# Landmark attention with a SiLU MLP: landmark scores as full-array products from batch 2 on, their exp in four pieces, exp(C) of batches 2 and 3 transposed by DMA, and a new order of the work

## The chip, the cores and the metric

The kernel runs on one core of a Trainium2 chip. The metric is the device time of one execution in microseconds (us). The core has a matrix engine (PE, with its weight loads shown as PEld), a vector engine (DVE), a scalar engine that evaluates functions by table (ACT), GpSimd (POOL) and a synchronisation engine (SP). In this kernel POOL issues the loads from memory, SP issues the DMA transposes and nearly all stores. Products land in PSUM, of which the kernel uses eight banks, and are copied from there by ACT or DVE.

## What is computed

Eight batches, eight heads, 576 positions, head size 64. Attention goes through 32 landmarks (means of 18 neighbouring positions); the result runs through a two-layer MLP with SiLU.

```python
m = 32; scale = 1.0 / np.sqrt(D)
q_lm = q.reshape(B, H, m, S // m, D).mean(axis=3)
k_lm = k.reshape(B, H, m, S // m, D).mean(axis=3)
A = sm(q, k_lm)            # sm: softmax of scale * a @ b.T
Bm = sm(q_lm, k_lm)        # 32 x 32 for each head
C = sm(q_lm, k)
Z = Bm.T / (norm_1(Bm) * norm_inf(Bm) + 1e-06)
for _ in range(6):
    Z = 2 * Z - Z @ Bm @ Z
x = A @ Z @ C @ v          # then heads are put side by side: 4608 x 512
h = x @ w_in               # 512 x 2048
out = (h * sigmoid(h)) @ w_out
```

## The kernel before

**Layout.** The heads of a batch lie in two groups (g = 0, 1) of four. A tile with heads and landmarks on its partitions has 4 x 32 = 128 of them. Positions are counted as landmark times 18 plus j.

**Order.** The kernel doesn't issue its work line by line. It describes some 1,500 pieces of work as `Op`s with a name such as `sb.3` (the landmark scores of batch 3), engines and estimated durations, dependencies, a priority and the PSUM banks needed. `Plan.run` (line 83) then places them engine by engine with a small model of durations, and the instructions are emitted in that order. The table `ORDER` (line 19) shifts priorities of single pieces by name; it is a list of numbers found by a search. Each engine works through its own list in order, so a piece that waits holds up all that stand behind it on that engine. While nothing else is ready in the first 45 us, PE gets filler products out of a zero tile (`zer`).

**Attention of one batch** (`attn`, line 540). For batches 0 to 2 (`NTR`) q and k are transposed on PE (`tr`, line 566) and copied out (`trc`); from batch 3 on SP transposes them by DMA (`xt`, line 590). The landmarks come from products with the identity in batches 0 and 1 (`lms`) and from batch 2 on from a tree of sums on DVE over the transposed q and k (`lra` to `lrd`, line 626), then a product with `fold` (`ltr`, line 646) and a copy into `lmT` (line 655). `fold` adds the halves and writes the sum to both halves of the partitions, so that `lmT` holds each landmark twice, on partitions 0 to 63 and 64 to 127.

`sb` (line 660) then makes the scores of the landmarks: for each group and each head one 32x32 product over 64 partitions, on a part of the array, eight in all. `pb` (line 677) takes the exp of these 128 x 64 scores in one ACT instruction. DVE sums, inverts and multiplies (`pbs`, `pbr`, `bmx`), PE sums columns (`csb`), DVE takes the norm; a block-diagonal square (`f0`) and six Newton steps follow (`ns` on PE, `nsd` on DVE, line 738).

`A` and `C` (lines 752, 797) are 16 products each with 64x32 parts of the array; ACT takes their exps (`Ax`, `Cx`, lines 768 and 813), PE sums those of A (`S`), ACT takes the logarithm and the exp of its negative (`Ln`, `Rs`), DVE multiplies (`etn`). The exps of C (tile `ce`) have to be transposed into `ct` before they multiply v. There are two ways: for `b < NCT`, with `NCT = 4`, PE transposes six blocks for each group (`ctm`, line 828) and ACT or DVE copies them out (`ctc`); for later batches SP transposes by DMA (`ct`, line 840). Then `cv` (line 848) makes C @ v on 96x64 parts, `zt` multiplies with Z, and `m` (line 895) with w_in on 64x32 parts.

**MLP.** `h` (line 927) multiplies `m` with the normalised exps of A, 16 blocks of 512 columns, with the remaining columns in `hx`; ACT applies SiLU (`g`, `gx`, line 940). The second layer (`layer2_pair`, line 1009) takes seven products `p1` to `p7` of 8 x 256 columns in place of eight, with sums of inputs on DVE (`ss`) and copies and additions of the results (`c1`, `c11`, `c22`, ...) into `ost`, from where SP stores. Pieces of the second layer stand between those of attention and of the first layer, so that PE has work while ACT is behind. SiLU and exp need different tables on ACT, so batches are taken in pairs: exps of batches 2 and 3, SiLU of 2 and 3, and so on.

**Transfers that exclude each other.** Loads come from POOL, for batch b+1 after batch b-1 has read its buffers. A DMA transpose is held back until the loads of the next v have landed (all but the last), and loads are held back for transposes. For C that is line 842, for the loads line 1125:

```python
xs + [prev.get("cv")] + v_ops.get(b + 1, [])[-2:-1], p0 + 20, lag=XLAG)]
...
gate = last[b - 1].get("xts", [])[-2:-1]
if b - 2 >= NCT:
    gate = gate + last[b - 2]["cts"][:1]
load_qk(b, 100.0 * b - 150, p["qk_read"], gate)
load_v(b, 100.0 * b - 149, [p["cv"]], gate)
```

Of the kernel before, what the change touches and what calls it, by code (L numbers as in the profile page):

```python
# [10 lines left out]
AF = mybir.ActivationFunctionType  # L11
# [5 lines left out]


ORDER = {
    "ns41.0": (259.18, 0), "mc21.0": (3218.2, 0), "mc31.0": (2171.9, 0), "tr19.1": (3337.5, 0),  # L20
    "lms0012.1": (4834.7, 0), "lms0112.1": (37.404, 0), "f0.1": (4487.7, 0),
    "Ax00.1": (418.45, 0), "Ax11.1": (120.61, 0), "etn1.1": (2471.6, 0), "Cx10.1": (6.1051, 0),
    "p3@5020.0": (591.27, 0), "tr10.2": (10.512, 0), "tr114.2": (-3277.8, 0),
    "lrb1.2": (92.182, 0), "ctm00.2": (-264.09, 0), "Cx11.2": (-1.6117, 0), "h12.1": (-10.003, 0),
    "c12@5100.0": (-2223.6, 0), "etn0.3": (-32.094, 0), "Ax10.3": (-1.1964, 0),
    "ctm10.3": (-212.55, 0), "ctc10.3": (1.228, 0), "mc01.3": (-72.297, 0), "m3.3": (-1035.6, 0),
    "p5@5200.0": (92.525, 0), "c12@5200.0": (-420.82, 0), "p3@5220.0": (291.71, 0),
    "c12@5220.0": (1822.7, 0), "wc.4": (385.62, 0), "m1.4": (5190.6, 0), "hx8.3": (-4.4068, 0),
    "p6@5300.0": (9579.2, 0), "p4@5300.0": (125.87, 0), "stf0.5": (79.994, 0), "C.5": (164.91, 0),
    "m3.5": (1570.1, 0), "p2@5400.0": (14.101, 0), "p4@5400.0": (-0.02249, 0),  # L30
    "Ax11.6": (-36.172, 0), "Cx10.6": (565.87, 0), "p6@5500.0": (-0.10422, 0),
    "ltr1.7": (-211.67, 0), "pbs.7": (230.47, 0), "bbd.7": (541.69, 0), "Rs0.7": (163.07, 0),
    "etn1.7": (-1755.9, 0), "hx0.6": (4199.5, 0), "p2@5740.0": (89.123, 0),
}


# [264 lines left out]
def act_us(n):  # L301
    return 0.06 + 0.00083 * n
# [6 lines left out]
def mm_us(n, count=1):  # L309
    return count * max(n / 2400 + 0.0025, 0.028)  # L310
# [3 lines left out]
def kernel(  # L314
# [9 lines left out]
    nc = tc.nc  # L324
    B, H, S, Dh = q.shape
    L = 32
    J = S // L
# [6 lines left out]
    NG = 2  # L334
# [3 lines left out]
    sc = 1.0 / float(Dh) ** 0.5  # L338
    SW = 128 + L
    NPE = 2  # L340
    NTR = 3
    MERGE = False
    WM = False
    NCT = 4
    XLAG = 3.0
    LOADS = "k1 q1 v0 w0 w1 w2 w3 o0 o1 o2 o3 v1".split()

# [8 lines left out]
    def bank(o, i=0):  # L356
        return banks[o.slot[i]]
# [33 lines left out]
    def mm(out_ap, lhsT, rhs, start=True, stop=True):  # L391
        nc.tensor.matmul(out=out_ap, lhsT=lhsT, rhs=rhs, start=start, stop=stop,  # L392
                         skip_group_check=True)
# [15 lines left out]
    A = P.add  # L409
# [74 lines left out]
    def consts(e):  # L484
# [13 lines left out]
        out=idb, in_=idb, compare_op=OP.is_equal, fill=0.0, base=0, pattern=[[-1, 128]],  # L498
        channel_multiplier=1), [c0], -99)
    for i, x in enumerate(LOADS):  # L500
        p, n = -95 + i, int(x[1])
# [38 lines left out]
    def attn(b):  # L540
        qk, qT, vs = qk_r[b % 2], qT_r[b % 2], v_r[b % 2]
        lm, lmT = lm_r[b % 2], lmT_r[b % 2]
        p0 = 100.0 * b
        prev = last.get(b - 1, {})
        prev2 = last.get(b - 2, {})
        me = last[b] = {}
# [3 lines left out]
        cr = b == 0  # L550
# [4 lines left out]
        if on_pe:  # L555
            blocks = {}
            me["qk_read"] = []
            for t in (1, 0):
                todo = [(g, jp) for g in range(NG) for jp in range(JP)]
                for i, n in STEPS[b]:  # L560
                    part = todo[i:i + n]

                    def tmm(e, t=t, part=part, key=(t, i)):
                        ps = bank(blocks[key]).bitcast(BF)
                        for n, (g, jp) in enumerate(part):
# [4 lines left out]
                    o = blocks[t, i] = A(f"tr{t}{i}.{b}", [("PE", mm_us(128, len(part)))], tmm,  # L570
                                         [qk_ops[b, t, part[0][0]], qk_ops[b, t, part[-1][0]], cid],
                                         p0 + 7 + (1 - t) * 0.5, psum=1)
# [9 lines left out]
        else:  # L582
# [3 lines left out]
            for t in (1, 0):  # L586
                for g in range(NG):
# [3 lines left out]
                            out=qT[:, t, g], in_=qk[:, t, g].rearrange("p j d -> p (j d)")),  # L591
# [10 lines left out]
        for t in (1, 0):  # L602
            if lm_pe:
                for g in range(NG):
                    for j0 in range(0, J, 6):
                        def lms(e, t=t, g=g, j0=j0):
                            ps = bank(me["lms", t])
                            for j in range(j0, j0 + 6):
# [3 lines left out]
                        o = A(f"lms{t}{g}{j0}.{b}", [("PE", mm_us(Dh, 6))], lms,  # L612
                              [qk_ops[b, t, g], cid] + ([] if first else [(me["lms_", t], 0.0)]),
                              p0 + 4 + 0.01 * j0 + 0.1 * g, psum=1 if first else 0, crit=True)
# [8 lines left out]
            else:  # L623
# [5 lines left out]
                if on_pe:  # L629
                    me["qk_read"] += blocks_of[t]  # L630
                x = lr("ra", 1024, red[:, :, 0:4], src[:, :, 0:4], src[:, :, 4:8],
                       qt_ops[t, 0] + qt_ops[t, 1] + tree[0])
                x = lr("rb", 512, red[:, :, 0:2], red[:, :, 0:2], red[:, :, 2:4], [x])
                x = lr("rc", 256, red[:, :, 0], red[:, :, 0], red[:, :, 1], [x])
# [22 lines left out]
        lmT_all = [lmT_ops[0], lmT_ops[1]]  # L657


        def sbm(e):  # L660
            ps = bank(me["sb"])
            for g in range(NG):
                for h in range(4):
                    mm(ps[L * h:L * h + L, g * L:(g + 1) * L], lmT[0:64, 0, g, L * h:L * h + L],
                       lmT[0:64, 1, g, L * h:L * h + L])
        ready = [l1_done.get(b - 2)] + prev.get("cts", []) + [prev.get("etn0"), prev.get("etn1")]
        if not cr:
            ready += sum(qt_ops.values(), [])
        ready = [x for x in ready if x is not None]
        me["sb"] = A(f"sb.{b}", [("PE", 0.2)], sbm, lmT_all + prev2.get("zt", []), p0 + (6 if cr else 11), psum=1,  # L670
                     tiled="q", crit=cr)
        pb, pbs = pb_r[b % 2], pbs_r[b % 2]
        bm, bmt = bm_r[b % 2][:, 0], bm_r[b % 2][:, 1]
        bbd = bbd_r[b % 2]
        sr = st_r[3 * (b % 2):3 * (b % 2) + 3]
        grp = "x0" if MERGE and b < 2 else f"x{b}"
        pb_op = me["pb"] = o = A(f"pb.{b}", [("ACT", act_us(64))],
                                 lambda e: nc.scalar.activation(
            out=pb, in_=bank(me["sb"])[:, 0:NG * L].rearrange("p (g l) -> p g l", g=NG),
            func=AF.Exp, scale=sc / (J * J)), [me["sb"]], p0 + 12, table="exp", group=grp,  # L680
            crit=cr).reads(me["sb"])
        pb_op.early = ready

        def chain(nm, us, emit, deps, prio=13):
# [505 lines left out]
```

## Time and profile before

| | |
|---|---|
| median of 4 runs | 250.94 us (250.38 to 252.05) |
| the profiled execution, its own time | 250.33 us |
| its span in the profile | 248.2 us |
| ACT, SiLU of the first layer (128 of 512 columns) | 65.8 us busy |
| PE, first layer (256 products of 512 columns) | 61.8 us busy |
| PE, filler products (94) | 15.8 us busy |
| PE, transposes of `ce` (48, batches 0 to 3) | 3.9 us busy |
| PE, landmark scores `sb` (64 products of 32 columns) | 1.8 us busy |
| ACT, exp `pb` (8) | 1.9 us busy, 233 ns each |
| SP, DMA transposes of `ce` into `ct` (8, batches 4 to 7) | 2.5 us from issue to landing, median |
| SP, DMA transposes of q and k (20) | 3.4 us from issue to landing, median |
| POOL, loads of v (24) | 12.1 us from issue to landing, median |

The span runs from the first to the last instruction of the program on the core; the execution's own time is 2.1 us longer. Busy times of PE overlap each other, since a product begins before the one before it has left the array: the distance from one start to the next tells what a product costs in a stream. The changes of ACT's table cut the span into stretches: SiLU of batch 0 begins at 33.7 us, the exps of batches 2 and 3 at 63.8, their SiLU at 89.8, the exps of 4 and 5 at 111.7, their SiLU at 137.1, the exps of 6 and 7 at 167.7, their SiLU at 190.5. The last product of PE ends at 244.3, after which the last results are added up and stored.

### The profile page before, as it was taken

What the parts mean: (1) busy time and instruction counts of PE and PEld (TensorE: products, weight loads), DVE (VectorE), ACT (ScalarE), POOL (GpSimd) and SP (SyncE); (2) the same over time, 40 slices, a digit from 0 to 9 for tenths busy, and PEclk for the clock granted to TensorE, in tenths of its full rate; (3) what the DMA queues carried; (4) which work ended last, traced back from release to release, by engine and by line L of the source; (5) the groups of instructions that cost most, each with busy time, mean ns of one, the idle gap of its engine ahead of it and who ended that gap; (6) DMA issues with size and microseconds to landing.
All of it is one profiled execution on the core that took longest, in us unless ns stands there. A gap on an engine that the chain in (4) does not pass through costs nothing.

```text
span 248.2 us, 7196 instructions
## 1 busy us (share of the span) xinstructions
PE 241.8 (97%) x2846; PEld 174.3 (70%) x2846; DVE 169.7 (68%) x430; ACT 182.8 (74%) x431; POOL 37.2 (15%) x63
## 2 busy tenths in 40 slices
PE   8999999999999999999999999999999999999993
PEld 6877665546877765567886564698876576688982
DVE  2376866596979886948999774489988384066421
ACT  2598998399886999996757979767679977822320
POOL 8436723200050022001300050000000000000000
PEclk9999999999999999999999999999999999999999
DMA  6999999999999699994995999674360033032333
GB/s 99 203 200 200 202 207 206 207 234 162 182 148 223 153 149 202 162 166 92 159 233 151 195 161 234 125 161 99 85 147 5 3 85 81 6 84 68 106 81 91
DMA packets 52482, 35.73 MB, mean 144 GB/s; under 512 B 33377, under 2 KB 43873, under 8 KB 52449
## 3 DMA queue, kind: packets, MB, share of 16 engines
q0 software_dynamic: 15264, 18.35, 44.7%
q1 hardware_dynamic: 36896, 16.66, 30.7%
q8 instruction: 22, 0.36, 0.6%
q10 hardware_dynamic: 288, 0.26, 0.4%
q14 instruction: 12, 0.09, 0.1%
HBM read 36.70 MB, written 9.44 MB: 186 GB/s over the span
## 4 chain that ended last, share of the span: by engine, by line
PE 86%; DMA 6%; ACT 3%; DVE 2%; issue 1%; POOL 0%; DVEq 0%; POOLq 0%; ACTq 0%
PE ps L392 83%; DMA qT<-qk 4%; DMA qk<-in_q_dram 3%; PE ps L566 2%; ACT ln L778 1%; DVE red L626 1%; ACT ln L782 1%; PE ps L828 1%; ACT ct L402 1%; ACT et L768 1%; ACT L940 1%; POOL qk L445 0%; DVE ost L1063 0%; ACT gm L940 0%; DVE ost L404 0%
## 5 line engine op out<-in xcount | busy, mean ns | idle before, releaser
L392 PE MATMUL ps<-etn,m 128*128 128x512 bf16 (+1 forms) x512 | 69.3, 286 | 0.1
L940 ACT ACTIVATE gm<-ps 128x512 f16<-128x512 f32 x128 | 65.8, 660 | 1.1 <-PE ps L392 0.9
L392 PEld LDWEIGHTS <-gm 128*128 128x128 f16 x512 | 48.2, 98 | 11.4 <-issue 2.4
L392 PE MATMUL ps<-w_out_sb,gm 128*128 128x256 f16 (+1 forms) x392 | 53.5, 281 | 0.0
L392 PEld LDWEIGHTS <-m 128*128 128x128 bf16 x512 | 32.5, 98 | 24.5 <-issue 2.3
L402 ACT COPY ost<-ps 128x256 f32<-128x256 f32 (+1 forms) x57 | 22.1, 388 | 33.8 <-PE ps L392 32.2
L392 PEld LDWEIGHTS <-ss 128*128 128x128 f16 x408 | 38.9, 98 | 7.1 <-issue 1.5
L1063 DVE TENSOR_TENSOR ost<-ost,ps 128x256 f32<-128x256 f32 x51 | 21.3, 417 | 27.3 <-PE ps L392 21.4
L392 PE MATMUL ps<-wt,ss 128*128 128x256 f16 x272 | 34.0, 273 | 0.0
L738 DVE SCALAR_TENSOR_TENSOR st<-st,ps 128x320 bf16<-128x320 bf16 (+3 forms) x54 | 21.6, 406 | 8.6 <-PE ps L392 8.3
L404 DVE CAST m<-ps 128x512 bf16<-128x512 f32 x31 | 20.0, 684 | 5.0 <-PE ps L392 4.5
L402 ACT CAST m<-ps 128x512 bf16<-128x512 f32 x33 | 17.9, 602 | 4.2 <-PE ps L392 4.2
L392 PE MATMUL ps<-w_out_sb,ss 128*128 128x256 f16 x136 | 17.6, 273 | 0.0
L392 PE MATMUL ps<-zer 128*128 128x256 bf16 x94 | 15.8, 304 | 1.1 <-DVE zer L485 1.1
L451 POOL DMA_DIRECT2D qk<-in_k_dram x7 | 5.0, 715 | 77.9 <-DMA qT<-qk 36.3
L458 POOL DMA_DIRECT2D v<-in_v_dram x24 | 14.0, 591 | 18.0 <-PE ps L392 11.0
L813 ACT ACTIVATE ce<-ps 128x288 bf16<-128x288 f32 x32 | 12.8, 412 | 5.2 <-PE ps L392 5.2
L392 PE MATMUL ps<-wt,gm 128*128 128x256 f16 x120 | 15.6, 273 | 0.0
L392 PE MATMUL ps<-st 128*128 128x160 bf16 (+1 forms) x96 | 14.4, 224 | 0.1
L1028 DVE TENSOR_TENSOR ss<-gm 128x1024 f16<-128x1024 f16 x15 | 10.2, 685 | 5.2 <-ACT gm L940 5.2
L778 ACT ACTIVATE ln<-ps 128x288 f32<-128x288 f32 x32 | 12.0, 435 | 1.6 <-PE ps L392 1.4
L402 ACT COPY qT<-ps 128x640 bf16<-128x640 bf16 (+1 forms) x13 | 8.5, 695 | 5.9 <-PE ps L566 5.9
(90 smaller groups left out, 328.0 us busy)
## 6 DMA issues: line engine op xcount, KB each, us to landing
out_dram<-ost SPq DMA_DIRECT2D x138, 64.0 KB, 1.8
v<-in_v_dram POOLq DMA_DIRECT2D x24, 192.0 KB, 12.1
qk<-in_k_dram POOLq DMA_DIRECT2D x7, 576.0 KB, 8.2
qk<-in_q_dram POOLq DMA_DIRECT2D x7, 576.0 KB, 11.4
w_out_sb<-in_moe_w_out_dram POOLq DMA_DIRECT2D x4, 512.0 KB, 11.3
w_in_sb<-in_moe_w_in_dram POOLq DMA_DIRECT2D x4, 256.0 KB, 8.8
w_in_sb<-in_moe_w_in_dram POOLq DMA_DIRECT2D x8, 128.0 KB, 7.2
qk<-in_k_dram POOLq DMA_DIRECT2D x2, 288.0 KB, 4.3
```

What stands on the lines that cost most here:

```text
L392: nc.tensor.matmul(out=out_ap, lhsT=lhsT, rhs=rhs, start=start, stop=stop, skip_group_check=True)
L402: nc.scalar.copy(out=out, in_=in_)
L404: nc.vector.tensor_copy(out=out, in_=in_)
L451: lambda e, t=t, src=src: nc.gpsimd.dma_start(out=qk_r[b % 2][:, t].rearrange("p g j d -> p g (j d)"), in_=src[b].rearrange("(g h) (l j) d ...
L458: lambda e, a=a: nc.gpsimd.dma_start(out=v_r[b % 2][a * L:(a + 1) * L, :, :], in_=v[b].rearrange("h (l a x) d -> a l h (x d)", l=L, a=VA)[ ...
L566: nc.tensor.transpose(out=ps[:, n * 128:(n + 1) * 128], in_=qk[:, t, g, 2 * jp:2 * jp + 2, :].rearrange("p j d -> p (j d)"), identity=idb)
L738: nc.vector.scalar_tensor_tensor(out=s2[:, g0:g1, lo:SW], in0=s[:, g0:g1, lo:SW], scalar=2.0, in1=ps[:, 0:NG * SW].rearrange("p (g x) -> p ...
L778: lambda e, g=g, c=c, ln=ln: nc.scalar.activation(out=ln[:, c], in_=bank(me["S", g, c])[:, 0:HS], func=AF.Ln),
L813: nc.scalar.activation(out=ce[:, :, 0:VP].rearrange("p (i c) (a l) -> p c a i l", c=2, a=VA)[:, c], in_=bank(me["C"], 2 * g + c)[:, 0:HS]. ...
L940: lambda e, dc=dc, cell=cell: nc.scalar.activation(out=gm[:, dc, :], in_=bank(cell["o"]), func=AF.Silu),
L1028: lambda e, o_=o_[:, k], x=x[:, k], y=y[:, k], op=op: nc.vector.tensor_tensor(out=o_, in0=x, in1=y, op=op), dep, 850.0 + prio / 100)
L1063: nc.vector.tensor_tensor(out=out_, in0=x, in1=y, op=OP.add)
```

## The change

1. `SBF = 2`: from batch 2 on `sb` makes one full-array product for each group, `lmT[:, 0, g]` with `lmT[:, 1, g]`, 128 partitions by 128 x 128. That holds the scores of all pairs of heads of the group; those of the same head are the four 32x32 blocks on the diagonal. As each landmark stands twice on the partitions, the sums are twice as large.
2. `pb` then takes the exp of the four diagonal blocks with four ACT instructions of 32 partitions x 64 columns, with half the scale.
3. `NCT = 2`: batches 2 and 3 transpose `ce` by DMA from SP as batches 4 to 7 do. With that the loads of batches 4 and 5 have to wait for the first such transpose of batches 2 and 3, and these transposes for the v loads of batches 3 and 4.
4. `ORDER` is a new list.

```diff
-    "ns41.0": (259.18, 0), "mc21.0": (3218.2, 0), "mc31.0": (2171.9, 0), "tr19.1": (3337.5, 0),
...
+    "tr09.0": (11.858, 0), "f0.0": (2417.6, 0), "nsd20.0": (1178, 0), "stf1.0": (616.27, 0),
...
+    SBF = 2
     MERGE = False
     WM = False
-    NCT = 4
+    NCT = 2
...
+        whole = b >= SBF
+
         def sbm(e):
             ps = bank(me["sb"])
             for g in range(NG):
+                if whole:
+                    mm(ps[:, g * 128:(g + 1) * 128], lmT[:, 0, g], lmT[:, 1, g])
+                    continue
                 for h in range(4):
                     mm(ps[L * h:L * h + L, g * L:(g + 1) * L], lmT[0:64, 0, g, L * h:L * h + L],
                        lmT[0:64, 1, g, L * h:L * h + L])
...
-        me["sb"] = A(f"sb.{b}", [("PE", 0.2)], sbm, lmT_all + prev2.get("zt", []), p0 + (6 if cr else 11), psum=1,
-                     tiled="q", crit=cr)
+        me["sb"] = A(f"sb.{b}", [("PE", mm_us(128, 2) if whole else 0.2)], sbm, lmT_all + prev2.get("zt", []), p0 + (6 if cr else 11), psum=1,
+                     tiled=None if whole else "q", crit=cr)
...
+            for h in range(4):
+                r = slice(L * h, L * h + L)
+                nc.scalar.activation(
+                    out=pb[r], in_=ps[r, 0:256].rearrange("p (g x) -> p g x", g=NG)[:, :, r],
+                    func=AF.Exp, scale=sc / (2 * J * J))
+        pb_op = me["pb"] = o = A(f"pb.{b}", [("ACT", act_us(64) * (4 if whole else 1))], pbe,
+                                 [me["sb"]], p0 + 12, table="exp", group=grp, crit=cr).reads(me["sb"])
```

In the instruction lists of the two kernels PE has 36 weight loads of `lmT` less, 48 products of 32 columns less and 12 of 128 columns more; 24 transposes of `ce` less; 6 fillers less. ACT has 24 small exps in place of 6, one copy of `ct` in place of six, three more copies of `lmT` and three fewer of `qT`; DVE takes up most of what ACT gives away in copies. SP has four more transposes. POOL's list is the same. The order of pieces differs on every other engine.

## The prediction

> **What bounds the kernel now.** I read the page first, then the stretches between ACT's changes of table, then PE in order of time, and last the queues of SP and POOL.
>
> ```profile
> span 248.2 us, 7196 instructions
> PE 241.8 (97%) x2846; PEld 174.3 (70%) x2846; DVE 169.7 (68%) x430; ACT 182.8 (74%) x431; POOL 37.2 (15%) x63
> PE 86%; DMA 6%; ACT 3%; DVE 2%; issue 1%; POOL 0%; DVEq 0%; POOLq 0%; ACTq 0%
> ```
>
> The second line is busy time, the third the chain that ended last: PE carries it. A busy PE is modelled and overlaps itself, so it doesn't prove that PE streams. The stretches and the starts do (columns: stretch; its length, then PE, PEld, DVE, ACT, POOL busy; clock, DMA, GB/s):
>
> ```profile
> 0.00:34.35 34.35, 32.80 (x517) 24.96 (x518) 20.55 (x72) 24.71 (x62) 19.76 (x35) 1.00 1.09 183
> ...
> 61.50:88.40 26.90, 26.32 (x371) 20.34 (x369) 23.77 (x68) 22.25 (x60) 3.14 (x5) 1.00 0.98 167
> 88.40:110.40 22.00, 22.00 (x219) 12.84 (x217) 15.19 (x33) 21.92 (x44) 3.15 (x5) 1.00 1.06 186
> ...
> 189.20:244.30 55.10, 55.05 (x515) 42.35 (x513) 26.34 (x52) 31.06 (x67) 0.00 (x0) 1.00 0.23 61
> ```
>
> Up to 34 us PE looks busy only because 94 filler products (out of zer) stand there: the limit is the chain of batches 0 and 1, with ACT busy 24.7 of 34.4 us. From 34 to 244 us PE is the limit; in 88 to 110, the SiLU of batches 2 and 3, ACT is full as well.
>
> PE in order of time, batch 2 and its surroundings (start, length, instructions, idle before):
>
> ```profile
> 61.51 0.22 PE L392 MATMUL ps<-lmT 64*32 64x32 bf16 x8
> 61.66 1.05 PE L392 MATMUL ps<-w_out_sb,gm 128*128 128x256 f16 x8
> ...
> 67.42 0.50 PE L828 MATMUL ps<-idb,ce 128*128 128x128 bf16 x6
> 67.75 0.27 PE L392 MATMUL ps<-bbd 128*128 128x128 bf16 x2
> 67.86 0.50 PE L828 MATMUL ps<-idb,ce 128*128 128x128 bf16 x6
> 68.20 1.04 PE L392 MATMUL ps<-w_out_sb,gm 128*128 128x256 f16 x8
> 69.16 0.44 PE L392 MATMUL ps<-qT,lmT 64*32 64x288 bf16 x16
> 69.53 1.05 PE L392 MATMUL ps<-wt,ss 128*128 128x256 f16 x8
> ...
> 72.44 0.41 PE L392 MATMUL ps<-et,hmask 128*128 128x288 bf16 x2 [0.58 <-DVE st L738]
> ```
>
> The cost is the distance from start to start, not the length. Six transposes of ce: 0.33. Two full products of 128 columns (bbd): 0.11. The scores sb: 0.15 plus the entry into the tiled array; that entry shows at 68.20, where eight products take 0.96 up to a tiled run instead of the usual 0.87, so 0.09. An isolated sb thus costs 0.24. The last line is the largest stop after 34 us.
>
> The queues (SP, then POOL):
>
> ```profile
> 61.50 5.71 SPq L590 DMA_TRANSPOSE qT<-qk  x4
> 68.01 15.78 SPq L1005 DMA_DIRECT2D out_dram<-ost  x16
> 83.97 6.40 SPq L590 DMA_TRANSPOSE qT<-qk  x4
> ```
>
> ```profile
> 68.45 0.70 POOL L451 DMA_DIRECT2D qk<-in_k_dram  x1 [18.17 <-PE ps L828]
> 69.15 0.71 POOL L451 DMA_DIRECT2D qk<-in_q_dram  x1
> 71.94 1.74 POOL L458 DMA_DIRECT2D v<-in_v_dram  x3 [2.08 <-PE ps L392]
> ```
>
> The loads of batch 4 start at 68.45, those of its v at 71.94 (after cv of batch 2), and only at 83.97 does SP transpose batch 4's q and k: a transpose waits for the second load of v.
>
> **What the Trainium skill says.** "TensorEngine Tiling (Array Packing)", Key Properties: changing the tiling mode drains the array. The trace agrees: 0.09 us in, about 0.10 out. "TensorE: Matmul & The Clock Gate", Back-to-back issue gap: warm, N columns take N/2.4 + 2.5 ns; for 128 that is 56 ns, the trace has 0.11 us for two. "DMA: Bandwidth & Descriptors", Issuing engines are not separate DMA queues: all DMAs run on the same 16 engines and interleave; the DMA share of about 1 in the stretch from 61.5 to 88.4 fits. So four more transposes meet a busy DMA.
>
> **The change, part by part.**
>
> *Transposes of ce.* Batches 2 and 3 lose 4 groups of 6: 0.33 + 0.34 + 0.34 + 0.33 = 1.34 us of PE, all in the stretch where PE is the limit. Also 4 copies of ct (two took 1.50 us on ACT, so 3.0 us), which lay beside PE.
>
> *Scores as full products.* In three of the six batches (2, 3, 5) sb stands alone (0.24); in 4, 6 and 7 it joins a tiled run and costs 0.04. That is 0.84 against 6 x 0.11 = 0.66. But the new order breaks tiled runs elsewhere: from the first block of layer 1 that runs without fillers (h6 of batch 0) I count 66 changes of array mode before and 65 after. Costed that way: 6 x (0.11 - 0.04) = +0.42, less 0.10 for the one change. With -1.34, and -0.14 for one Newton step of batch 1 that now stands before h6, PE's work from h6 on falls by 1.16 us.
>
> *Four exp pieces.* One pb took 0.225 us. The skill's "ScalarE: Activation LUTs", What ACT_TABLE_LOAD costs, gives 186 ns plus 0.83 per column and an overlap of 93 ns between neighbours; with the trace's 0.225 I estimate 0.225 + 3 x 0.132 = 0.62 us. Bounds for four: 0.56 (they overlap as pb and the next exp at 12.78 and 12.92 do) and 0.90 (no overlap). 0.4 us longer per batch, in front of sum, reciprocal, product and csb on PE: some 1.7 us from pb to csb. Behind pb on ACT wait the first exps of C or A. The least PE work between sb and csb in the new order is 4.1 us (batch 3; before 2.5), so it is covered: 0. If the cover fails it costs 6 x 0.4 = 2.4.
>
> *ct by DMA for batches 2 and 3.* New waits: SP's ct of batch 3 waits for the second v load of batch 4; behind it on SP stand the q and k transposes of batch 4 and eight stores. The loads of batch 4 wait for the first ct of batch 2 (about 70.5: its exps end near 68, and a ct lands 2.5 us after issue), so 2 us later; the v loads follow cv of batch 2, now about 74.5 to 75 against 71.56. Loads and stores took 15.5 us from 68.45 to 83.97, so v is there at about 86; at the median of 12.1 us from issue to landing of v, at 88. Then the second ct of batch 3 lands 1.25 + 2.5 us later: 89.8 to 91.9. PE reaches cv of batch 3 at about 91.6: from h6 on I added, in the new order, each block's usual distance in the trace (0.43 for one h, 0.87 for one product p, 0.14 for a Newton step, 0.645 for cv, 0.1 for each change of mode), which gives 91.0, plus 0.6 for stops. So the wait lies between 0 and, with v's longest landing of 14.7, 3 us; I take 0.4. Batches 4 and 5 do the same already, without a stop on PE.
>
> *Order.* Start: 88 fillers instead of 94 (-0.66) and 0.34 more real work before h6: -0.3. ACT has there one ct copy and three qT copies less and one lmT more, about 2.1 us; if all of that is on the path the start gains 2.1, if not, and batch 0's later Newton chain (h0 stands 1.06 later) counts, it loses 0.7. The stop of 0.46 us before A of batch 4, where DVE waited for batch 5's transposes (DMA qT<-qk in the chain, 108.5 to 113.2), goes: that reduction now stands on DVE behind the norm of batch 4. The stop at 72.44 stays: it comes from batch 3's transposes, bound by loads that do not move.
>
> Sum against the profiled execution: -1.16 - 0.3 - 0.46 + 0.4 = -1.5; span 248.2 to 246.7, its own time 250.33 to 248.8. The median of the runs shown, 250.94, lies 0.6 above that execution, so 249.4.
>
> **Rivals.** (A) Forecast, 249.4. (B) The ACT work taken from the start is all on its path: -2.1 instead of -0.3, 247.6. For it: ACT is nearly unbroken from 13 to 32 us. Against it: only six fillers fewer. (C) The order's gain returns as new short stops elsewhere and only the transposes remain, partly: 250.5. For it: ACT and PE are both full in 88 to 110. (D) Slower: v of batch 4 lands late, so ct and cv of batch 3 stop PE for 3 us; the q and k transposes of batch 4, behind ct on SP, then stop DVE in front of copies of m of batch 3 for 1 more: -1.9 + 4.0 gives 253.0. From 88 us on, each us of later landing costs one; slower than 0.5% from about 91. For it: DMA is full there. Against it: batch 5 ran so with 1.5 us to spare. That sb or pb do nothing of what they say is excluded by the instruction lists.
>
> **How the numbers follow.** What a measurement can tell is about 0.5%, 1.25 us. A 0.50 (0.35 below 249.69, 0.15 within), B 0.17, C 0.11, D 0.22: faster 0.52, same 0.26, slower 0.22. Range 247.2 to 252.9: B's value less the last of its gain, up to D's; A's own is 248.2 to 250.4.
>
> **What would show it.** Right: six stretches with two 128-column products of lmT, no L828 at 67 to 82; PE starts at cv of batch 3 without idle; h6 of batch 0 near 35.0. Wrong: PE idle named after DMA ct<-ce or v at about 91 (D); first SiLU near 31.7 instead of 33.7 (B); more PE stops than the 0.58 and 0.29 of before (C).

## The result, and the profile after

The changed kernel takes 250.08 us in the median (249.02 to 252.41) beside 250.85 us for the kernel before, ratio 0.9965 with a 95% interval of 0.9951 to 0.9979. Compared once more later (the run after_again below) the ratio was 0.9987 (0.9967 to 1.0008). Weighted by their widths the two give 0.9972 (0.9960 to 0.9984), some 0.7 us less: a small gain, inside the 0.5% that the prediction named as no change and gave a chance of 0.26, against 0.52 for a larger gain. The forecast was 249.4 us, a gain of 1.5 us: the time lies in its range, the gain is half of it. The 250.5 of rival C lies nearer to the measured time than the forecast does.

The profiled execution of the changed kernel took 249.02 us, the lowest of its times, against 250.33 for the one of before. So the difference of these two profiles, 1.3 us, is more than the change is worth, and below I set several profiles beside each other.

The page of the changed kernel: its span, the busy time of the engines, the chain that ended last.

```profile
span 247.3 us, 7085 instructions
PE 239.8 (97%) x2780; PEld 171.4 (69%) x2780; DVE 168.5 (68%) x432; ACT 180.8 (73%) x443; POOL 37.3 (15%) x63
PE 86%; DMA 7%; ACT 2%; POOL 1%; SPq 1%; DVE 1%; issue 1%; POOLq 0%; DVEq 0%
```

PE carries the chain as before. It has 2.0 us less busy time, and the span is only 0.9 us shorter. The stretches between ACT's changes of table, for the exps and then the SiLU of batches 2 and 3 (columns as in the prediction):

```profile
60.80:86.10 25.30, 24.60 (x314) 18.83 (x312) 22.12 (x64) 20.41 (x63) 3.14 (x5) 1.00 0.97 176
86.10:108.90 22.80, 22.15 (x230) 12.92 (x229) 14.90 (x32) 22.40 (x46) 3.15 (x5) 1.00 0.97 171
```

In the second stretch PE is now idle for 0.65 of 22.8 us; before, it was idle for none of 22.0. PE in order of time in the changed kernel:

```profile
59.86 0.28 PE L396 MATMUL ps<-lmT 128*128 128x128 bf16 x2
59.98 1.06 PE L396 MATMUL ps<-etn,m 128*128 128x64 bf16 x18
...
69.96 0.65 PE L396 MATMUL ps<-et,hmask 128*128 128x288 bf16 x4
71.32 1.03 PE L396 MATMUL ps<-wt,ss 128*128 128x256 f16 x8 [0.70 <-DVE ost L1081]
72.19 0.30 PE L396 MATMUL ps<-st 128*128 128x160 bf16 x2
```

```profile
88.04 1.11 PE L396 MATMUL ps<-etn,m 128*128 128x512 bf16 x18 [0.57 <-ACT gm L958]
...
90.57 1.50 PE L396 MATMUL ps<-etn,m 128*128 128x512 bf16 x6
91.99 0.86 PE L396 MATMUL ps<-v,ct 96*64 96x128 bf16 x24
```

The two full products of the scores take 0.12 us from start to start, as reckoned. `cv` of batch 3, at 91.99, starts without idle. The stop at 72.44 of before is now at 71.32, in front of a product `p5` of the second layer. Both hang on the same landing: DVE stands idle until the transposes of batch 3 are there, and what PE waits for stands behind that on DVE (DVE, before and changed):

```profile
70.50 0.69 DVE L626 TENSOR_TENSOR red<-qT 128x1024 f16<-128x1024 bf16 x1 [0.74 <-DMA qT<-qk]
```

```profile
70.24 0.69 DVE L630 TENSOR_TENSOR red<-qT 128x1024 f16<-128x1024 bf16 x1 [1.34 <-DMA qT<-qk]
```

At 88.04 there is a stop that before did not have. The queues of SP and POOL:

```profile
60.98 5.72 SPq L594 DMA_TRANSPOSE qT<-qk  x4
66.81 3.51 SPq L858 DMA_TRANSPOSE ct<-ce  x2
70.42 9.94 SPq L1023 DMA_DIRECT2D out_dram<-ost  x16
85.45 2.55 SPq L858 DMA_TRANSPOSE ct<-ce  x2
88.10 6.34 SPq L594 DMA_TRANSPOSE qT<-qk  x4
```

```profile
71.37 0.70 POOL L455 DMA_DIRECT2D qk<-in_k_dram  x1 [21.50 <-DMA ct<-ce]
...
74.82 1.73 POOL L462 DMA_DIRECT2D v<-in_v_dram  x3 [2.05 <-PE ps L396]
```

The loads of batch 4 start 2.9 us later than before (the prediction had 2) and those of its v at 74.82, as the prediction had it, and the `ct` transposes of batch 3 are issued at 85.45 and about 86.7. SP had nothing to do from 80.4 to 85.45; what held the `ct` back was v of batch 4, which thus landed at about 85.4 and not, as the prediction had it, between 86 and 88.

Laid against the order of the two kernels, the starts of PE's pieces split the time from the start to the end. Rows: h6 of batch 0 is the first block after the fillers; "stops" is the distance from h6 to the last product p less the work that lies between them at the usual distances; "end" is from the start of that last p to the end of the span.

```
us                              h6 of batch 0   last p    stops   end
before                               35.32      243.21     2.88   5.0
before, once more                    35.77      244.56     3.78   5.0
changed                              34.03      241.51     3.62   5.8
changed, once more                   34.30      243.12     4.96   7.4
same order, exps on all rows         34.81      241.88     3.21   7.6
same order, exps by columns          33.97      241.53     3.70   5.8
same order, two exps left out        34.67      242.20     3.66   5.7
```

The work of PE between h6 and the last p is 205.01 us before and 203.86 after, -1.15. It is reckoned with the prediction's distances; outside the stops told of below, the starts of PE's pieces follow it to within 0.2 us at each piece. Not all of the column "stops" is idle time: of the 2.88 us of before the trace shows 0.9 as idle, of the 3.62 of the changed kernel 1.4, and the rest is small delays. Taken without those distances, as the time from h6 to the last p less PE's idle time, the mean is 207.1 us in the two profiles of before and 206.3 in the five others: 0.8 less. So the saved work is 0.8 to 1.15 us, by the way of reckoning.

### The profile page after: what moved, and what is told of

It is laid out like the page before. It is cut to its first block, busy times and chain, and to the rows that moved or that the text cites. A ratio compares the mean times of both kernels' runs of the same rounds, so it can differ in the third digit from the quotient of the medians.

```text
span 247.3 us, 7085 instructions
## 1 busy us (share of the span) xinstructions
PE 239.8 (97%) x2780; PEld 171.4 (69%) x2780; DVE 168.5 (68%) x432; ACT 180.8 (73%) x443; POOL 37.3 (15%) x63
## 4 chain that ended last, share of the span: by engine, by line
PE 86%; DMA 7%; ACT 2%; POOL 1%; SPq 1%; DVE 1%; issue 1%; POOLq 0%; DVEq 0%
PE ps L396 84%; DMA qk<-in_k_dram 4%; DMA qT<-qk 2%; PE ps L570 2%; ACT gm L958 1%; POOL qk L449 1%; DMA out_dram<-ost 1%; SPq L1023 1%; PE ps L846 1%; ACT gx L981 0%; DVE ost L1081 0%; DVE red L630 0%; ACT pb L695 0%; DVE st L756 0%; SPq L594 0%
## 5 line engine op out<-in xcount | busy, mean ns | idle before, releaser
L396 PE MATMUL ps<-etn,m 128*128 128x64 bf16 (+1 forms) x512 | 69.5, 286 | 0.6 <-ACT gm L958 0.6
L958 ACT ACTIVATE gm<-ps 128x512 f16<-128x512 f32 x128 | 66.7, 653 | 1.3 <-PE ps L396 1.0
L406 ACT COPY ost<-ps 128x256 f32<-128x256 f32 (+1 forms) x55 | 21.2, 388 | 37.1 <-PE ps L396 34.1
L455 POOL DMA_DIRECT2D qk<-in_k_dram x7 | 5.0, 715 | 80.4 <-DMA ct<-ce 40.5
L396 PEld LDWEIGHTS <-st 128*128 128x128 bf16 x96 | 8.5, 97 | 5.9 <-issue 1.1
```

The source lines that it names most:

```text
L406: nc.scalar.copy(out=out, in_=in_)
L455: lambda e, t=t, src=src: nc.gpsimd.dma_start(out=qk_r[b % 2][:, t].rearrange("p g j d -> p g (j d)"), in_=src[b].rearrange("(g h) (l j) d ...
L958: lambda e, dc=dc, cell=cell: nc.scalar.activation(out=gm[:, dc, :], in_=bank(cell["o"]), func=AF.Silu),
```

## The experiments

**Parts and order apart.** parts_old_order has the changed kernel's parts with the table `ORDER` of before; order_old_parts has `ORDER` of the changed kernel with the old parts. The edit of order_old_parts against the changed kernel:

```diff
-    SBF = 2
+    SBF = 8
...
-    NCT = 2
+    NCT = 4
```

> All three new parts (full-array scores, four exps, ct of batches 2 and 3 by DMA), planned with the ORDER list of before. Theory 1 (what was gained is the start, which hangs on ORDER, and PE work): the start is that of before (94 fillers, first filler-free block h6 of batch 0 near 35.3 us, not 34.0) and PE's work from there on, counted with the distances of the trace, is 0.7 us less than before; stops are those of an order not searched for these parts, 0 to 2 us more: 250.1 to 252.3, so no faster than before by more than 0.3 %. Theory 2 (the parts themselves carry the gain): about 0.9 us faster than before, as after.

> None of the new parts (SBF = 8, NCT = 4), planned with the ORDER list of after. Theory 1: the start is that of after (88 fillers, h6 of batch 0 near 34.0 us, 1.3 us earlier than before), but PE's work from there on is 1.6 us more than before (83 changes of array mode against 66): the same as before within 0.5 us, or slower by up to 2 if stops come on top. Theory 2: the start stays at 35.3, since it hung on something else than ORDER, and the kernel is slower by 1.6 us or more.

Measured: 256.31 us, ratio 1.0203 (1.0164 to 1.0242) for the parts with the old order, 253.67 us, ratio 1.0114 (1.0082 to 1.0146) for the new order with the old parts. Both are slower than either kernel. What PE waited for with the old order, and PE's largest stop with the old parts (the view of waits of the first, PE in order of time of the second):

```profile
PE ps L393 <- DVE st L753: 1.7, 3, 0.8
...
PE ps L393 <- ACT m L403: 0.5, 1, 0.5
PE ps L393 <- DVE st L735: 0.5, 1, 0.5
PE ps L393 <- ACT et L783: 0.4, 1, 0.4
```

```profile
90.32 0.41 PE L396 MATMUL ps<-w_in_sb,zt 64*32 64x512 bf16 x8 [1.72 <-DVE m L408]
```

PE's stops add up to 9.3 us in the first and 5.4 in the second, against 2.9 to 5.0 in the two kernels. The work of PE is 204.31 and 206.59 us, so the parts save what they should, and their saving is lost many times over in an order found for other parts. In parts_old_order the pieces wait behind each other in small portions, none over 1 us. ACT also changes its table 12 times in place of 8, since with this list a SiLU of the remaining columns (`gx`) falls between the exps of batches 2 and 3 (ACT in order of time):

```profile
72.67 1.28 ACT L978 ACT_TABLE_LOAD   x1
...
79.03 1.28 ACT L1158 ACT_TABLE_LOAD   x1
```

The other two extra loads are at 182.6 and 186.2. How much of the lost time these four loads cost was not tried. Both theories on the size of the single parts missed. What stands: the start hangs on the order. h6 of batch 0 is at 35.20 with the old order and at 34.25 with the new.

**The old scores in the new order.** The order of the changed kernel is held; only what `sb` and `pb` emit goes back to eight 32x32 products and one exp.

```diff
-                if whole:
+                if False:
...
-            if not whole:
+            if True:
```

> The order of after held piece by piece, but the scores again as eight 32x32 products and one exp for each batch. All six stand alone among full-array work in this order. Theory 1 (the price of an isolated tiled group, 0.24 us against 0.11): PE has 0.8 us more, after + 0.8, about as before. Rival (the exps decide: four of them take 0.90 us in the trace of after against 0.22, 4 us of ACT in all): ACT is relieved, stops shrink, and the time is after + 0.2 or less.

Measured: 250.65 us, ratio 0.9995 (0.997 to 1.002), 0.2 to 0.75 us more than the two comparisons of the changed kernel. The last p begins 208.84 us after h6; in the five profiles of the changed order above it is 207.07 to 208.82, and 0.77 us of the 208.84 are one stop at 147.78 that these do not have. So the time alone doesn't settle the price of the scores, but the starts do (PE in order of time, this run):

```profile
59.49 1.03 PE L396 MATMUL ps<-etn,m 128*128 128x512 bf16 x4
60.45 0.22 PE L396 MATMUL ps<-lmT 64*32 64x32 bf16 x8
60.60 1.07 PE L396 MATMUL ps<-etn,m 128*128 128x64 bf16 x18
```

From the start of the last product ahead of `sb` to the first one behind it the old scores take 0.46 us here (60.14 to 60.60), the full products 0.33 in the changed kernel (59.65 to 59.98). At five of the six places the difference is 0.13 to 0.14, at the sixth 0.10: 0.8 us in all, as reckoned. The four exps do not make the stop at 88: it stays with a single exp.

**Two of the stops, by moving pieces.** two_moves takes the landmark sums of batch 3 on DVE behind a Newton step of batch 2, one copy on ACT behind a SiLU, and one copy from ACT to DVE.

```diff
     order = P.run()
+    move('lra0.3', 'nsd00.2')
+    move('lrb0.3', 'lra0.3')
+    move('c21@5120.0', 'g1.2')
+    move('ztc.2', 'stf0.3', 'DVE')
```

> The order of after with four pieces moved: on DVE the first two sums of batch 3's q landmarks go behind the addition c11 and the first Newton step of batch 2; on ACT the copy c21 of the pair before goes behind the second SiLU of batch 2, and the copy ztc of batch 2 goes to DVE. Theory 1 (the stops of 0.86 us at 71.3 and 0.73 us at 88.0 are head-of-line waits on DVE and ACT): both shrink to 0.2 or less, PE's last product comes 1.0 to 1.4 us earlier, time after - 1.0 or so, the fastest of all. Rival (DMA and ACT bind, a stop only moves to the next piece): less than 0.4 us faster than after.

Measured: 250.38 us, ratio 0.9979 (0.9957 to 1.0001); the stops are 3.68 us. The rival of the expectation holds. The stop at 88 is still 0.50 us of idle time, and the stop before p5 is gone, but this one stands in its place, at the product that makes the landmarks (PE in order of time):

```profile
74.28 0.27 PE L396 MATMUL ps<-rs,fold 128*128 128x256 f16 x1 [0.68 <-DVE st L756]
```

**ct later still.** What would the prediction's rival D cost? In late_ct the four transposes of q and k of batch 4 go ahead of both `ct` of batch 3 on SP.

```diff
+    move('xt01.4', 'xt00.4')
+    move('ct0.3', 'xt01.4')
+    move('ct1.3', 'ct0.3')
```

> The changed kernel in its held order, but on SP the four q and k transposes of batch 4 stand ahead of both ct transposes of batch 3. In the changed kernel these ct were issued at 85.45 and 86.7, landed by about 89.3, and PE began cv of batch 3 at 91.99 without a wait: a slack of 2.7 us. The four transposes took 6.34 us. Theory 1 (what rival D of the prediction said, each us later costs one once the slack is used): ct lands 6.3 us later, cv stops PE for 3.6 us, and the time rises by 3.6 us, ratio to the kernel before about 1.011. Theory 2 (other work regains it, because ACT limits this stretch too and empties its backlog during the stop): the stop is there but the time rises by less than half of it, under 1.8 us, ratio under 1.004.

SP, then PE, of this run:

```profile
85.82 6.46 SPq L594 DMA_TRANSPOSE qT<-qk  x4
92.38 2.72 SPq L858 DMA_TRANSPOSE ct<-ce  x2
```

```profile
90.99 1.50 PE L396 MATMUL ps<-etn,m 128*128 128x512 bf16 x6
95.32 0.53 PE L396 MATMUL ps<-v,ct 96*64 96x128 bf16 x12 [2.83 <-DMA ct<-ce]
96.44 0.85 PE L396 MATMUL ps<-v,ct 96*64 96x128 bf16 x12 [0.60 <-DMA ct<-ce]
```

Measured: 254.25 us in the median of four executions, ratio 1.0123 (1.007 to 1.0176); two more executions took 256.32 and 257.02. The four are 3 to 4 us over the changed kernel for a `ct` 6.9 us later (issued at 92.38 in place of 85.45). Theory 1 holds for the stop: the waits at `cv` are 2.83 and 0.60, where it had 3.6 together. But the sum of the stops rises by more than that, from 3.6 to 8.5. The rest is the clock: 0.8 us after PE had work again, the granted clock fell to 0.50 for 3.4 us (columns as in the prediction).

```profile
96.10:99.50 3.40, 3.06 (x34) 2.06 (x35) 2.06 (x6) 0.90 (x2) 2.89 (x5) 0.50 0.81 131
```

From the second half of `cv` to the block of 512 columns behind the remaining ones PE takes 3.78 us here (96.44 to 100.22), against 2.37 in the changed kernel. That is 1.4 us more, and 3.4 and 1.4 make up the 4.9. The executions fit: 252.35 us came with a mean clock of 0.995, 254.2 to 254.5 with 0.988 to 0.990, the two long ones with 0.984 and 0.983. So rival D's mechanism is right, and its price, one for one, is too low by what the clock adds. In the changed kernel the stop was 3.6 us away (the first `cv` came 2.94 us after the issue of its `ct` here, so that it could have begun at 88.4 there, and began at 91.99).

**Is it ACT that makes the stop at 88?** no_rs3 leaves out two exps of batch 3 on ACT ahead of the change of table.

```diff
+            if o.name in ("Rs0.3", "Rs1.3"):
+                continue
             r = o.emit(e)
```

> The changed kernel in its held order without the two exps of batch 3 that turn the log of the row sums into the reciprocal (L800), so that batch 3 is normalised wrongly: this part of the computation is left out. ACT then has 1.2 to 1.4 us less between 79.7 and the change of table at 86.1. Theory 1 (the new stop of 0.6 to 0.7 us before the third h of that stage, released by ACT gm, comes from the amount of work on ACT ahead of the change of table): the table load starts 1.0 to 1.2 us earlier, the stop goes, and the kernel gains 0.6 us, ratio about 0.994. Theory 2 (ACT waits for PE's m products there, which stand directly ahead of the h): the load starts at most 0.4 us earlier, a stop of 0.3 or more stays, ratio about 0.995 to 0.9965.

ACT in order of time, first the changed kernel, then no_rs3:

```profile
82.16 0.70 ACT L800 ACTIVATE ln<-ln 128x576 f32<-128x576 f32 x1
...
83.19 0.68 ACT L800 ACTIVATE ln<-ln 128x576 f32<-128x576 f32 x1
83.78 1.54 ACT L406 CAST m<-ps 128x512 bf16<-128x512 f32 x3
...
86.10 1.28 ACT L958 ACT_TABLE_LOAD   x1
87.39 2.55 ACT L958 ACTIVATE gm<-ps 128x512 f16<-128x512 f32 x5
```

```profile
84.07 1.56 ACT L406 CAST m<-ps 128x512 bf16<-128x512 f32 x3 [1.12 <-PE ps L396]
...
86.42 1.28 ACT L958 ACT_TABLE_LOAD   x1
87.71 2.56 ACT L958 ACTIVATE gm<-ps 128x512 f16<-128x512 f32 x5
```

In the changed kernel ACT looks full right up to the table load. With the two exps gone, ACT has 1.12 us of idle and still waits for PE's products `m`. Counted from h6 (34.03 and 34.67) the load comes at 52.07 and 51.75, 0.32 us earlier, and the stop keeps its size (0.69 after 0.73). Theory 2 holds: what ends last there is a chain, `m` on PE, its copies, the load of 1.28 us, the first SiLU, the bank that it frees. (The h that stops is the fifth of its stage; the expectation calls it the third.) The median is 249.43 us, ratio 0.9966 (0.9946 to 0.9987).

**Both stops at once.** six_moves adds to two_moves a later place for an addition `ss`, for the landmark product `ltr0` and for a product `p4`; start_of_3 leaves the stretch at 88 alone and orders the pieces around the landmarks of batch 3.

```diff
+    move('ss00@5120.0', 'nsd10.2')
+    move('ltr0.3', 'cv0.2')
+    move('p4@5120.0', 'm3.2')
```

> The changed kernel in its held order with seven instructions moved: the four moves of the run two_moves, and the first addition of ss (DVE) behind the last step of batch 3's q landmarks, ltr0 of batch 3 (PE) behind cv of batch 2, and a product p4 (PE) behind the last m of batch 2. Theory 1 (the stops at 71 to 74 and at 88 are faults of order that can be mended one by one): both go, 1.3 to 1.7 us less stops than the changed kernel, ratio about 0.990 to 0.992. Theory 2 (other engines are as full as PE there, so that the time comes back at the next piece): stops fall by less than 0.5 us, ratio 0.995 to 0.998.

```diff
+    move('lra0.3', 'nsd00.2')
+    move('lrb0.3', 'lra0.3')
+    move('lrc0.3', 'nsd10.2')
+    move('lrd0.3', 'lrc0.3')
+    move('ss00@5120.0', 'lrd0.3')
+    move('ltr0.3', 'cv0.2')
+    move('sb.3', 'ns30.2')
```

> The changed kernel in its held order with seven moves around the late transposes of batch 3 alone: the two first additions of its q landmarks (DVE) behind the first norm step of batch 2 and the two next behind the second, the first addition of ss behind those; ltr0 (PE) behind cv of batch 2, sb of batch 3 behind the next norm step. The stretch from 80 to 90 us is left as it is. Theory 1 (a better order hides the landing of these transposes): the stops of 0.86 and 0.15 at 71 to 74 go, at most 0.2 new, the rest stays: stops 2.6 to 2.9 instead of 3.6, ratio to the kernel before 0.993 to 0.995. Theory 2 (what is bound by the landing at about 70.2 returns at the next piece, as in the runs two_moves and six_moves): stops 3.3 or more, ratio 0.996 to 0.999.

Measured: six_moves 250.74 us, ratio 0.9996 (0.997 to 1.0022), stops 4.2; start_of_3 249.76 us, ratio 0.9967 (0.9945 to 0.9989), stops 4.2. In six_moves, where a product p4 stands between m and h and the change of table comes at 85.71, the stop at 88 shrinks to 0.16, and m3 stops for 0.57 us at 84.4 instead (both by the usual distances). In both, the stops at 71 to 73 are replaced by one at 74 to 75; in start_of_3 (PE in order of time):

```profile
73.43 0.86 PE L396 MATMUL ps<-v,ct 96*64 96x128 bf16 x24
74.22 0.28 PE L396 MATMUL ps<-rs,fold 128*128 128x256 f16 x1
74.97 0.30 PE L396 MATMUL ps<-st 128*128 128x160 bf16 x2 [0.46 <-ACT lmT L406]
```

The Newton step at 74.97 uses the PSUM bank of the landmark product at 74.22 and waits for ACT to copy that out. In both runs the stops did not fall, as theory 2 said, though the ratio of six_moves is above its range. Its reason is not shown here: this stop is one of the bank, made by my move. start_of_3 is not told apart from the changed kernel by these intervals. No version of mine is shown to beat it.

**Why four exps take 0.90 us.** pb_all_rows lets each piece work on all 128 partitions with its head's columns, pb_columns on 128 partitions and 16 columns that no other piece writes.

```diff
-                    out=pb[r], in_=ps[r, 0:256].rearrange("p (g x) -> p g x", g=NG)[:, :, r],
+                    out=pb, in_=ps[:, 0:256].rearrange("p (g x) -> p g x", g=NG)[:, :, r],
...
+                    out=pb[:, :, 8 * h:8 * h + 8],
+                    in_=ps[:, 0:256].rearrange("p (g x) -> p g x", g=NG)[:, :, 8 * h:8 * h + 8],
```

> The changed kernel, but each of the four exp pieces of a pb works on all 128 partitions with its head's columns, so that only the last head's columns stay in the result: this part of the computation is changed. It asks why the four pieces took 0.90 us, 0.215 to 0.225 each, without the overlap that other exps in a row show. Theory 1 (it is the 32 partitions at four different places): the four now overlap, 0.56 to 0.65 us together. Theory 2 (it is the small size, or the same target tile): still 0.86 to 0.90. The time stays that of the changed kernel either way.

> The changed kernel, but each of the four exp pieces of a pb works on all 128 partitions and 16 of the 64 result columns, which are not the columns the scores need: this part of the computation is changed. No piece writes what another wrote, unlike in the run pb_all_rows, where ACT waited for its own exps. Theory 1 (32 partitions at four places hinder the overlap): the four overlap, 0.50 to 0.65 us together. Theory 2 (exps that read one bank of PSUM one after the other don't overlap, whatever their rows): 0.80 to 0.90.

ACT in order of time, `pb` of batch 2 in the changed kernel, in pb_all_rows, in pb_columns:

```profile
63.11 0.90 ACT L695 ACTIVATE pb<-ps 32x64 f32<-32x64 f32 x4
```

```profile
63.89 0.99 ACT L695 ACTIVATE pb<-ps 128x64 f32<-128x64 f32 x4
```

```profile
63.04 0.41 ACT L695 ACTIVATE pb<-ps 128x16 f32<-128x16 f32 x4
```

In the changed kernel each of these pieces takes about 215 ns and the next begins 11 to 12 ns after its end, with no wait on a semaphore between them. In pb_all_rows each piece writes what the last one wrote and ACT waited for itself, so that run decides nothing. In pb_columns the four, 190 ns each, take 0.41 us together: a step of 0.07, an overlap of 0.12. So exps that read one bank in a row can overlap, and theory 2 of that run falls. Whether it is the 32 partitions, that all four pieces write the same columns of different partitions, or that each has 64 columns and not 16, stays open: the run changed all three. Against the last speaks that in before a copy began at 63.92 while a `pb` of 128 x 64 ran from 63.80 to 64.02. Times of the two: 251.43 and 248.98 us, one execution each.

**Both kernels once more.**

> The changed kernel once more, for a second look at its start and its stops. In the first look h6 of batch 0 began at 34.03 and the last p at 241.51; six other kernels with the same order at the start have h6 at 34.0 to 35.0. Theory 1 (the forecast's sum with the corrections found: work -1.15, stops +0.7, start -0.3 to -0.8): h6 at 34.0 to 34.8, stops after it 3.2 to 3.7, ratio to the kernel before 0.995 to 0.998. Theory 2 (the first comparison was luck of the executions and the change is worth the -1.15 of work in full, or nothing): ratio under 0.995 or over 0.999.

> The kernel before once more, for a second look at its start and its stops. Theory 1 (the start hangs on the order): h6 of batch 0 at 35.0 to 35.5 as in the first look (35.32) and in the run with the old order (35.20), stops after it 2.7 to 3.1. Theory 2 (the later start was luck of that execution): h6 at or under 34.8.

Measured: the changed kernel 250.15 us, ratio 0.9987 (0.9967 to 1.0008), h6 at 34.30, stops 4.96; before 251.68 us in its one execution, h6 at 35.77, stops 3.78. The start agrees with theory 1, though 35.77 lies a little above its band. The stops of both lie above what I had allowed: the stop that waits for the transposes of batch 3 was 0.75 and 1.18 us in the two profiles of before, 0.86 and 1.05 in those of the changed kernel. It moves with the landing from one execution to the next, and one profile gives no size for it. The ratio lies between the two theories' ranges.

## Why the prediction was right, and where it was off

- *PE's work, -1.16.* Right as far as the starts in the trace bear it out: -1.15 with the prediction's distances, -0.8 by idle time. It comes from the 24 transposes, the price of an isolated tiled group (0.24 against 0.11, which the old scores in the new order show) and the count of mode changes.
- *Start, -0.3 (bounds -2.1 to +0.7).* Mis-sized. h6 is at 35.2 to 35.8 in three profiles with the old order. In all other runs, which have the new one, it is at 34.0 to 35.0, mean 34.4: -1.0. The fillers show only part of it. The gain lies where rival B looked for it, on ACT (from the start to the change to SiLU, before and changed, columns as in the prediction):

```profile
0.00:32.41 32.41, 30.95 (x503) 23.63 (x504) 18.61 (x69) 22.79 (x59) 19.04 (x34) 1.00 1.08 182
```

```profile
0.00:31.06 31.06, 29.69 (x498) 22.28 (x499) 20.05 (x72) 20.57 (x56) 18.65 (x34) 1.00 1.07 182
```

ACT has 2.2 us less to do ahead of that change, as the prediction counted, and the change comes 1.35 us earlier (1.54 in the second pair of profiles). So about two thirds of ACT's saving got through, where the forecast let almost none through and rival B all of it.
- *The stop before A of batch 4, -0.46.* Right that it goes: 0.36 and 0.61 in before, gone in every profile of the new order that holds the new parts. The 0.46 held 0.10 of a change of mode that the prediction counts with the work.
- *ct of batch 3, +0.4 (0 to 3).* No stop at `cv`. v of batch 4 landed earlier than estimated: the prediction took 83.97 as the end of the loads of before, but there the second load of v had landed at 79.80, and it was SP's stores that ran to 83.79. But the cost came in another place. Before, `cv` of batch 3 stood ahead of the products `m`, and a product `p3` (0.88 us) lay between the fourth and the fifth h of the stage, where PE waits for the change of table. In the new order `cv` stands at 92, the products p are used up ahead of 85, and the fifth h follows the fourth with only a Newton step between them: stop 0.73. That the later `ct` forced this order is read from the two orders, not tried; that the stop stays with the two exps on ACT left out, and with one exp for `pb`, is shown.
- *"The stop at 72.44 stays."* Right. Three attempts moved it; since in two of them the stop that came instead was made by the move itself, it isn't shown that no order can hide it.
- *Sum of the stops, -0.06.* Mis-sized, and in kind: it was made of the two named stops alone, and allowed for none that the new order brings. The one at 88 is such: 0.53 to 0.58 us of idle time in all five profiles of the changed order in the table, none in the two of before. For the sum, the mean of two profiles is 3.3 before; of those five it is 3.8: +0.5. The ranges overlap (2.9 to 3.8 and 3.2 to 5.0), so this figure is rough. Rival C named this (gains return as short stops), with the right sign and too much of it.
- *Four exps, 0.62 us, hidden.* They took 0.90, the upper bound, and were hidden: no stop of PE in the changed kernel's two profiles is put down to them, and one exp in their place (old_scores_held) made nothing faster. The cover of 4.1 us held.
- *The end, taken as unchanged.* Mis-sized too, put at nothing: the span ends 5.0 us after the start of the last p in both profiles of before, 5.7 to 6.0 in nine runs that have the `ct` of batches 2 and 3 on SP and 7.4 to 7.6 in two. SP's last stores, before and changed:

```profile
237.75 8.10 SPq L1005 DMA_DIRECT2D out_dram<-ost  x14
```

```profile
236.05 8.44 SPq L1023 DMA_DIRECT2D out_dram<-ost  x14
```

The last issue ends at 245.85 and 244.49, which is 2.64 and 2.98 us after the last p began. In the trace each store uses one of eight semaphores again and waits until its last user has landed. In before, the first store of the last results got one that was free at -0.2 (counted from the last p) and was issued at 0.65; in the changed kernel it got that of a store issued at -0.60, and left at 1.10. That costs 0.33 up to the last landing. After it SP checks the eight semaphores in a fixed order, 0.06 us each. In before the last landing is that of the eighth; in the changed kernel it is that of the fourth, and the four checks behind it cost 0.25. Another 0.2 in the closing code is open. order_old_parts has the late first store too (1.14) and lands last at 4.38, nearly as the changed kernel (4.42), but on the eighth semaphore, and its end is 5.3. So the late store comes with the order, and the 0.25 with the four more transposes, which move the stores on by four semaphores. In the two long ends SP's first store of the last results left at 2.88 and 3.20; why is not shown.

- *The clock.* No term of its own. The mean granted clock is a little lower in the changed kernel (0.9972 over 66 executions, 0.9987 over 124 of before), but in the two profiles of each kernel the clock is 1.00 as long as PE has work. In after_again, with a mean of 0.994, the lower clock stands behind PE's last product, which ended at 244.2:

```profile
247.70:250.50 2.80, 0.00 (x0) 0.00 (x0) 0.00 (x0) 0.00 (x0) 0.00 (x0) 0.50 0.17 47
```

There the low mean is a mark of a long end, not a cause.

The sum now: -1.15 of work, -1.0 at the start, +0.5 of stops and +0.75 at the end make -0.9 us; with the two long ends in the mean the end is +1.1, and the sum about -0.6. The two comparisons give -0.7. Against the forecast the start gave 0.7 us more, and stops and end took 1.3 to 1.7 us. That the time lies near the forecast is in part luck: these terms were off in opposite directions.

## What to carry to other kernels

When the bound engine runs at 97%, reckon a change in its work by distances from start to start, but don't forecast its stops from those that one profile shows: they are bound by chains through other engines, came back at another piece in each of three attempts here, and their sum differed by about 1 us between two executions of one kernel. A long stop can cost more than its length: in late_ct the clock put 1.4 us on top of 3.4. A part and the order found for it can't be priced apart: here each alone cost 1 to 2% where both together gained 0.3%, and the old list with the new parts even had four more changes of ACT's table. Where a chain at the start binds, ask how much of another engine's saving gets through, and don't settle on none or all of it. Look at what a piece that moves had been covering, and at the last stores as well, where a few more DMAs earlier on can shift which semaphore each one waits for.

## What the runs showed of the hardware

Four exps of 32 partitions x 64 columns in a row took 0.90 us, 215 ns each, without any overlap, where four of 128 x 16 took 0.41. The Trainium skill's "ScalarE: Activation LUTs", What ACT_TABLE_LOAD costs, has neighbours overlap by 93 ns; the second case comes near that (0.12), the first does not show it.

In late_ct PE stood idle for 2.83 us, worked for 0.53 and stood idle for 0.60; the granted clock then was 0.50 for 3.4 us, from 96.1 on, and 1.00 again behind that. The largest stop of order_old_parts, 1.72 us, was followed by no such fall: the clock there was 1.00 to the end.

The old scores in the changed order show the price of a short tiled group among full-array products: eight 32x32 products took 0.13 to 0.14 us more, from the product ahead to the one behind, than two full products of 128 columns.
